# Top-k attention and a GELU MLP on one core: a folded top-k search, softmax rows transposed by row halves ahead of the scores, and GpSimd divisions by two multiplications

## The chip, the cores and the metric

The kernel runs on one core of one Trainium2 chip. The metric is the device time of one execution in microseconds (us), the median of several runs. The engines are named as the profile names them: PE is TensorE (matmuls; PEld are its weight loads), DVE is VectorE, ACT is ScalarE, POOL is GpSimd, SP is SyncE, which here only issues transfers.

## The reference

The first block is attention with a top-k mask; the second is a two-layer MLP with exact GELU over the same tokens. All of q, k, v are float32; w_in and w_out come as 8-byte floats.

```python
batch, n_heads, seq, head_dim = (8, 8, 576, 64)     # q, k, v
n_tokens, d_model, d_ff = (4608, 512, 2048)         # x, w_in, w_out

scores = scale * np.matmul(q, k.transpose(0, 1, 3, 2))
kth = np.partition(scores, -32, axis=-1)[..., -32:-31]
scores = np.where(scores >= kth, scores, -1e9)
attn = np.exp(scores - np.max(scores, axis=-1, keepdims=True))
attn = attn / (np.sum(attn, axis=-1, keepdims=True) + 1e-9)
out = np.matmul(attn, v)
x = out.transpose(0, 2, 1, 3).reshape(4608, 512)
h = x @ w_in
g = 0.5 * h * (1 + erf(h / sqrt(2)))
result = g @ w_out
```

So for each of 64 heads and each of its 576 rows, the 32nd largest of 576 scores is the threshold. Only its value is needed, and the largest score for the exponent.

## The kernel before

**Items and slots.** Heads are taken in pairs. An item is one block of 128 query rows for both heads of a pair, so 128 partitions by 2 x 576 scores. The 64 rows that are left over in each head (576 = 4 x 128 + 64) of two pairs are put together in "last" items. A batch of 8 heads gives 18 items, 16 of the main kind and 2 last ones; all eight give 144 (`items`). The main loop `for n in range(ahead)` has a slot for each item and four more, and in slot n it works on items at different stages: scores of item n+2, search of item n, softmax and division of item n-1, transposes of item n-2, and the product with v of item n-3. The order of the instructions of each engine is the order in which the code issues them; nothing reorders them.

**What one slot issues.** `scores(n + 2)`: matmuls of the last 64 keys of both heads (`t_ps`, L290) and of the 512 main keys (`s_ps`, L294, 64 rows of the array for each head), and ScalarE's copies out of PSUM (L304, L305) into the tile `s`. `attend(n - 3)`: for every second main item, and for each last one, the product with v (`o`, L473 and L484); its copy into the ring `xT` is put on a list and issued by `copy_x()`. `transposes(n - 2)`: eight 128x128 transposes (L436) and one of the last keys (L418) through PSUM, copied to SBUF by ScalarE (L443, L419). `softmax(n - 1, e)` for the two heads e: Prelu pushes what is below the threshold far down (L386), Exp gives the weights and their sum (L387). `top_k(n)`: four rounds of VectorE's MAX8 (L347), which gives the eight largest of a row, and three of MATCH_REPLACE8 (L350), which takes them out; one of each for each head. `inverse(n - 1)`, a reciprocal on VectorE (L373) behind the last round. `threshold(n)` and `add_small(n - 1)`, tiny instructions on GpSimd (L362, L365, L379). `normalise(n - 1)`: the division of the rows of `s` by their sum, two GpSimd instructions (L399), in a few slots on VectorE.

**The MLP** is cut into pieces of some 0.86 us of TensorE work each, in one list. Eight pieces of the first layer (`h_ps`, L525) and eight of the second (`y_ps`, L561) take turns. `mlp(count)` issues the next pieces; a slot issues eight of them, four in slots 10 and 11. So an even slot has a product with v and the first layer, an odd one the second layer. The gelus (L536) of two first-layer units are released behind the sixth piece of the second-layer block (`GELU_AT = 5`) and issued to ScalarE at the next `run_gelus()`. Exp and Gelu each need a table load of their own on ScalarE (`ACT_TABLE_LOAD`).

**PSUM** has eight banks: `s` two, `l1` two (h), `l2` two (y), and the tag `tp` two, which are handed out in turn to `t_ps`, `o` and the transposes. A tile that gets a bank waits until the copy out of the tile before it in that bank is done.

**The first 20 slots** also bring the weights in: units of 8-byte floats come by DMA and are turned into float32 by ScalarE and GpSimd instructions (L190 to L225; L210 multiplies by 2**-13). Up to slot 9 TensorE gets dummy matmuls between its work (`keep_busy`). `START` is 10. Behind the last slot the pieces of the MLP that are left run by themselves.

**Loads.** q and k of a pair come in six transfers each (`load`, L99), the first pair's k by ScalarE's queue and the rest by SP's.

Of the kernel before, what the change touches and what calls it, by code (L numbers as in the profile page):

```python
# [8 lines left out]
TOPK = 32  # L9
# [5 lines left out]
def kernel(  # L15
# [19 lines left out]
    nc = tc.nc  # L35
# [49 lines left out]
    def raw_of(n, pair):  # L85
        return raws[n][pair % len(raws[n])]

    def load(n, pair, queue=None, queue2=None):
        if pair >= n_pairs:
            return  # L90
        queue = queue or nc.sync
        queue2 = queue2 or queue
        b, h0 = pair // NP, 2 * (pair % NP)
        t, src = raw_of(n, pair), sources[n]
        if n != "v":
            for e, a in ((0, 0), (0, 1), (1, 0), (1, 1)):
                at = e * D + a * SQ
                for lo, hi, c in ((0, S, 0),) if e == 0 else ((0, SM, 0), (SM, S, SM + TL)):
                    (queue if a == 0 else queue2).dma_start(  # L99
                        out=t[at : at + SQ, c : c + hi - lo].rearrange("p (j d) -> p j d", d=SQ),  # L100
                        in_=src[b, h0 + e, lo:hi, a * SQ : (a + 1) * SQ].rearrange(
                            "(j p) d -> p j d", p=SQ
                        ),
                    )
            return
        for e in range(2):
            queue.dma_start(
                out=t[:, 0:NM, e, :], in_=src[b, h0 + e, 0:SM].rearrange("(t p) d -> p t d", p=P)
            )
            queue2.dma_start(out=t[e * TL : (e + 1) * TL, NM, e, :], in_=src[b, h0 + e, SM:S])  # L110

    load("k", 0, nc.scalar)
    load("q", 0)
    make_identity(nc, ident)


# [36 lines left out]
    def load_weights(n, queue=None):  # L153

        queue = queue or nc.sync
        u = unit_in(n)
        if u is None:
            return
        src, r, c, dst = weights_of(u)
        if src.dtype == f32:  # L160
            for x in range(2):
                queue.dma_start(
                    out=dst[:, x], in_=src[(r + x) * P : (r + x + 1) * P, c : c + WS]
                )
            return


        half, i = src.bitcast(u16), ORDER.index(u)
        if i not in (2, 12, 14, 15):
            at = FT // 2 + 4 * (i % 2)  # L170
            t = w_out_sb[:, at : at + 4, :].rearrange("p (a b) n -> p a (b n)", a=2)
        else:
            t = stage.tile([P, 2, 2 * WS], f32, tag="words", name="words")
        for a in range(2):
            queue.dma_start(
                out=t[:, a].bitcast(u16)[:, 0 : 4 * WS - 1],
                in_=half[(r + a) * P : (r + a + 1) * P, 4 * c + 1 : 4 * (c + WS)],
            )
        words[u] = t

    def parts(u):

        t, dst = words[u], weights_of(u)[3].bitcast(i32)
        return t[:, :, 0::2], t.bitcast(mybir.dt.int16)[:, :, 2::4], t[:, :, 1::2].bitcast(i32), dst

    def weights_size(u):
        if u not in words:
# [18 lines left out]
    def weights_add(u):  # L206
        if u in words:
            w, _, below, d = parts(u)
            if on_pool(u):
                nc.gpsimd.tensor_scalar(  # L210
                    w.bitcast(i32), w.bitcast(u32), 2.0**-13, None, op0=ALU.mult
                )
            nc.gpsimd.tensor_tensor(d, d, below, op=ALU.add)
            if not ends_late(u):
                weights_end(u)
        made.add(u)
# [60 lines left out]

        return spread(t[:, e * TL :], step + (TL if e == 0 else -TL), TL)

    def scores(i):  # L280
        if i >= N:
            return
        pair, t = items[i]
        S_of[i] = s = work.tile([P, 2 * S], f32, tag="s", bufs=5, name="s")
        s_ps = ps.tile([P, 2, 512], f32, tag="s", bufs=1, name="s_ps")
        t_ps = ps.tile([P, 512], f32, tag="tp", name="t_ps")
        if t < NM:
            qk = qk_of[pair]
            lhsT = qk[:, t * P : (t + 1) * P]
            nc.tensor.matmul(t_ps[:, 0:P], lhsT=lhsT, rhs=qk[:, KT:], start=True, stop=True)  # L290
            for c in range(2):
                for e in range(2):
                    rows = slice(e * D, (e + 1) * D)
                    nc.tensor.matmul(  # L294
                        s_ps[:, e, c * 256 : (c + 1) * 256], lhsT=lhsT[rows, :],
                        rhs=qk[rows, KM + c * 256 : KM + (c + 1) * 256], start=True, stop=True,
                    )
            if i == 0:

                nc.scalar.activation(s[:, 0:SM], s_ps[:, 0], func=AF.Copy, scale=scale)  # L300
                nc.vector.tensor_scalar(s[:, SM : S + TL], t_ps[:, 0:P], scale, None, op0=ALU.mult)
                nc.scalar.activation(s[:, S + TL :], s_ps[:, 1], func=AF.Copy, scale=scale)  # L302
                return
            nc.scalar.activation(spread(s, S + TL, SM), s_ps, func=AF.Copy, scale=scale)  # L304
            nc.scalar.activation(s[:, SM : S + TL], t_ps[:, 0:P], func=AF.Copy, scale=scale)  # L305
        else:
            for r in range(2):
                qk = qk_of[pair + r]
                for e in range(2):
                    nc.tensor.matmul(  # L310
                        t_ps[half(r, e), r * TL : (r + 1) * TL],
                        lhsT=qk[:, SM + e * TL : SM + (e + 1) * TL],
                        rhs=qk[:, KT + e * TL : KT + (e + 1) * TL],
                        start=True, stop=True,
                    )

            for r in range(2):
                qk = qk_of[pair + r]
                for e in range(2):
                    rows = slice(e * D, (e + 1) * D)  # L320
                    nc.tensor.matmul(  # L321
                        s_ps[half(r, e), r, :], lhsT=qk[rows, SM + e * TL : SM + (e + 1) * TL],
                        rhs=qk[rows, KM:KT], start=True, stop=True,
                    )
            s2 = s.rearrange("p (r n) -> p r n", r=2)
            nc.scalar.activation(s2[:, :, 0:SM], s_ps, func=AF.Copy, scale=scale)
            nc.scalar.activation(
                s2[:, :, SM:S], t_ps[:, 0:P].rearrange("p (r n) -> p r n", r=2),
                func=AF.Copy, scale=scale,
            )  # L330

    def top_k(i, hooks):

# [5 lines left out]
            "den": work.tile([P, 2], f32, tag="den", name="den"),  # L339
            "rden": work.tile([P, 2], f32, tag="rden", name="rden"),  # L340
        }
        cur = [row(i, e) for e in range(2)]
        rest = work.tile([P, 2, S], f32, tag="rest", bufs=1, name="rest")
        n_op = 0
        for r in range(TOPK // 8):
            for e in range(2):
                nc.vector.max(st["top"][:, e, 8 * r : 8 * r + 8], cur[e])  # L347
            if r < TOPK // 8 - 1:
                for e in range(2):
                    nc.vector.match_replace(  # L350
                        rest[:, e], st["top"][:, e, 8 * r : 8 * r + 8], cur[e], LOWEST
                    )
                cur = [rest[:, e] for e in range(2)]
            if r in hooks:
                hooks.pop(r)()

    def threshold(i):

# [30 lines left out]
            accum_out=st["den"][:, e : e + 1],  # L389
        )  # L390

    def normalise(i, on_dve):

        if i < 0 or i >= N:
            return
        st = stat_of[i]
        for e in range(2):
            s = row(i, e)
            (nc.vector if e >= 2 - on_dve else nc.gpsimd).tensor_scalar(  # L399
                s, s, st["rden"][:, e : e + 1], None, op0=ALU.mult  # L400
            )

    pt_now = [None]
# [3 lines left out]
    def transposes(i):  # L407
# [35 lines left out]
            nc.scalar.copy(out=dst, in_=tp.rearrange("p (j n) -> p j n", j=NM))  # L443

        return [tails] + [lambda e=e: main(e) for e in range(2)]

    def copy_x():
        while copies:
# [173 lines left out]
    ready, left = [0], [0]  # L622

    eager = [False]
    staging = ExitStack()
    stage = staging.enter_context(tc.tile_pool(name="stage", bufs=1))

    load("k", 1)
    load("q", 1)
    for n in range(1, 3):  # L630
        load_weights(n)
# [7 lines left out]
            nc.tensor.matmul(warm[:, 0:P], lhsT=m, rhs=m, start=True, stop=True)  # L639

    keep_busy(WARM, idle)
    for pair in range(2):
        for piece in transpose_qk(pair):
            piece()
        if pair == 0:
            scores(0)
            scores(1)

# [6 lines left out]
    for pair in range(2, n_pairs):  # L657
        b, p = divmod(pair, NP)
        for at, piece in zip(first.get(pair, slots_of[b % 2][p]), transpose_qk(pair)):
            prep_in.setdefault(starts[b] + at, []).append(piece)  # L660
    ahead = N + 4
    for n in range(ahead):

        left[0] = 4 if n in (START, START + 1) else 8
        eager[0] = n > N
        if not waits(unit_in(n)):
            weights_add(unit_in(n))
        scores(n + 2)
        product = attend(n - 3)
        late = n > START  # L670
        if n <= START:
# [43 lines left out]
        if n < N:  # L715
# [2 lines left out]
                    piece()  # L718
                inverse(n - 1)

            top_k(n, {3: behind_searches})
        else:
            inverse(n - 1)
        threshold(n)
        u = unit_in(n + 1)

        normalise(n - 1, 2 if on_pool(u) else 0)

        if not waits(unit_in(n + 1)):
            weights_size(unit_in(n + 1))  # L730
# [8 lines left out]
    while done[0] < len(pieces):  # L739
        mlp(1)  # L740
        run_gelus()
    staging.close()


# [30 lines left out]
```

## Time and profile before

| | |
|---|---|
| time, median of 3 runs | 1621.87 us (1621.77 to 1622.47) |
| the profiled execution's own time | 1622.63 us |
| its span, first to last instruction | 1620.9 us |
| granted TensorE clock, mean | 0.987 |
| busy: PE, DVE, ACT, POOL | 98%, 90%, 71%, 41% |
| slots, from one first MAX8 to the next: 4 to 7 | 9.70 us each |
| the same, slots 12, 14, 15 and 16 | 12.2 us each |
| the same, slots 20 to 142, mean | 10.55 us |
| first MAX8 of slot 0; of slot 20; of slot 143 | 13.2; 227.1; 1525.0 us |

A line of a group reads: source line, engine, operation, output tile <- input tiles, shapes, count, then busy time in us, mean duration of one in ns, and the engine's idle time before them with what ended it. A line of a timeline has the start, the length, the engine, the line, the operation, the tiles and how many like instructions were merged. The duration of an instruction includes what the next one overlaps; where instructions follow each other without a pause, the time from start to start is the cost of one.

### The profile page before, as it was taken

The numbers are of one execution on the slowest core, as the hardware profiler recorded it, in microseconds if no ns is written. First come the engines' busy times: TensorE is split into PE (matmuls) and PEld (weight loads), VectorE is DVE, ScalarE is ACT, GpSimd is POOL, SyncE is SP. The second block draws the span as 40 slices with busy tenths as digits, with TensorE's granted clock in tenths as the row PEclk, the third lists the DMA queues.
The fourth block names the chain that finished last, engine by engine and source line by source line (L and its number), as shares of the span: only waits on it lengthen the run. The fifth ranks groups of instructions, "written<-read, shape, count | busy, mean of one in ns | idle before, by whom it ended". The sixth has DMA issues, their size and how long they took to land.

```text
span 1620.9 us, 25358 instructions
## 1 busy us (share of the span) xinstructions
PE 1588.7 (98%) x8864; PEld 1082.8 (67%) x8864; DVE 1460.1 (90%) x3108; ACT 1144.1 (71%) x2038; POOL 663.9 (41%) x758
## 2 busy tenths in 40 slices
PE   6899899999999999999999999999999999999999
PEld 5676476766666667776666667676666666666665
DVE  7999999999999999999999998999999999999800
ACT  4898787777777777777777777777777777777720
POOL 3886754333444333344333344333344333444400
PEclk7999999999999999999999999999999999999999
DMA  6533320011101211012100111002110101000000
GB/s 138 169 93 93 92 58 1 20 32 36 35 1 32 33 24 29 1 29 44 36 16 16 29 30 43 1 21 37 30 36 8 36 1 36 2 14 7 1 13 13
DMA packets 202640, 56.18 MB, mean 35 GB/s; under 512 B 193680, under 2 KB 193936, under 8 KB 202512
## 3 DMA queue, kind: packets, MB, share of 16 engines
q1 hardware_dynamic: 199968, 54.13, 14.5%
q8 instruction: 70, 1.15, 0.3%
q10 hardware_dynamic: 2544, 0.43, 0.1%
q14 instruction: 58, 0.48, 0.1%
HBM read 45.08 MB, written 9.44 MB: 34 GB/s over the span
## 4 chain that ended last, share of the span: by engine, by line
PE 87%; DVE 10%; DMA 1%; SPq 1%; issue 0%; POOL 0%; ACT 0%; DVEq 0%; ACTq 0%; POOLq 0%
PE y_ps L561 30%; PE h_ps L525 30%; PE o L473 8%; PE s_ps L294 7%; PE tp L436 7%; DVE top L347 5%; DVE rest L350 4%; PE t_ps L290 2%; PE o L484 1%; PE tp_t L418 1%; PE s_ps L321 1%; SPq L99 1%; DVE qk L255 1%; DVE s L399 0%; PE t_ps L310 0%
## 5 line engine op out<-in xcount | busy, mean ns | idle before, releaser
L347 DVE MAX8 top<-rest 128x8 f32<-128x576 f32 x864 | 609.2, 746 | 0.0
L525 PE MATMUL h_ps<-xT,w_in_sb 128*128 128x256 f32 (+1 forms) x2560 | 547.5, 361 | 0.0
L561 PE MATMUL y_ps<-w_out_sb,g 128*128 128x512 f32 x1152 | 545.0, 600 | 0.0
L399 POOL TENSOR_SCALAR s<-s,rden 128x576 f32<-128x576 f32 x278 | 477.1, 1726 | 8.6 <-DVE rden L373 8.0
L525 PEld LDWEIGHTS h_ps<-xT,w_in_sb 128*128 128x128 f32 x2560 | 432.7, 191 | 64.2 <-issue 14.8
L350 DVE MATCH_REPLACE8 rest<-top,rest 128x576 f32<-128x576 f32 x576 | 423.2, 742 | 0.0
L379 POOL TENSOR_SCALAR den<-den 128x2 f32<-128x2 f32 x144 | 32.1, 223 | 785.2 <-ACT s L387 784.8
L561 PEld LDWEIGHTS y_ps<-w_out_sb,g 128*128 128x128 f32 x1152 | 198.8, 191 | 187.0 <-issue 186.2
L304 ACT ACTIVATE s<-s_ps 128x1024 f32<-128x1024 f32 x127 | 130.7, 1029 | 177.4 <-PE s_ps L294 177.0
L387 ACT ACTIVATE s<-s,bias 128x576 f32<-128x576 f32 x288 | 223.3, 776 | 12.6
L386 ACT ACTIVATE s<-s,neg 128x576 f32<-128x576 f32 x288 | 224.1, 778 | 0.5 <-POOL neg L362 0.4
L443 ACT COPY pt<-tp 128x512 f32<-128x512 f32 x256 | 147.1, 575 | 101.9 <-PE tp L436 101.3
L350 DVE MATCH_REPLACE8 rest<-top,s 128x576 f32<-128x576 f32 x288 | 211.6, 742 | 0.0
L436 PEld LDWEIGHTS tp<-ident,s 128*128 128x128 f32 x1152 | 143.5, 142 | 89.3 <-issue 57.6
L347 DVE MAX8 top<-s 128x8 f32<-128x576 f32 x288 | 201.5, 741 | 0.0
L436 PE MATMUL tp<-ident,s 128*128 128x128 f32 x1152 | 174.2, 275 | 3.9 <-ACT pt L419 3.5
L473 PE MATMUL o<-pt,raw_v 128*64 128x256 f32 x1280 | 152.9, 385 | 0.5 <-ACT pt L443 0.5
L294 PE MATMUL s_ps<-qk 64*128 64x256 f32 x1024 | 150.8, 414 | 0.9 <-ACT s L302 0.5
L473 PEld LDWEIGHTS o<-pt,raw_v 128*64 128x64 f32 x1280 | 86.5, 137 | 64.5 <-issue 15.1
L294 PEld LDWEIGHTS s_ps<-qk 64*128 64x128 f32 x1024 | 91.1, 192 | 23.6 <-ACT s L302 0.8
L536 ACT ACTIVATE g<-h_ps 128x512 f32<-128x512 f32 x144 | 78.6, 594 | 37.8 <-PE h_ps L525 37.1
L387 ACT ACT_TABLE_LOAD x67 | 86.0, 1283 | 5.1
(72 smaller groups left out, 1002.9 us busy)
## 6 DMA issues: line engine op xcount, KB each, us to landing
raw_v<-in_v_dram SPq DMA_DIRECT2D x64, 128.0 KB, 2.4
out_dram<-y SPq DMA_DIRECT2D x31, 256.0 KB, 2.2
w_out_sb<-in_moe_w_in_dram SPq DMA_DIRECT2D x14, 511.8 KB, 4.9
w_out_sb<-in_moe_w_out_dram SPq DMA_DIRECT2D x10, 511.8 KB, 4.1
raw_q<-in_q_dram SPq DMA_DIRECT2D x64, 72.0 KB, 2.2
raw_k<-in_k_dram SPq DMA_DIRECT2D x62, 72.0 KB, 2.3
raw_q<-in_q_dram SPq DMA_DIRECT2D x64, 64.0 KB, 2.2
raw_k<-in_k_dram SPq DMA_DIRECT2D x62, 64.0 KB, 2.2
```

The lines of the kernel that those rows point to most:

```text
L294: nc.tensor.matmul(s_ps[:, e, c * 256 : (c + 1) * 256], lhsT=lhsT[rows, :], rhs=qk[rows, KM + c * 256 : KM + (c + 1) * 256], start=True, s ...
L304: nc.scalar.activation(spread(s, S + TL, SM), s_ps, func=AF.Copy, scale=scale)
L347: nc.vector.max(st["top"][:, e, 8 * r : 8 * r + 8], cur[e])
L350: nc.vector.match_replace(rest[:, e], st["top"][:, e, 8 * r : 8 * r + 8], cur[e], LOWEST)
L386: nc.scalar.activation(s, s, func=AF.Prelu, bias=st["neg"][:, e, 1:2], scale=1.0, alpha=STEEP)
L387: nc.scalar.activation(s, s, func=AF.Exp, bias=st["bias"][:, e : e + 1], scale=1.0, accum_out=st["den"][:, e : e + 1],)
L399: (nc.vector if e >= 2 - on_dve else nc.gpsimd).tensor_scalar(s, s, st["rden"][:, e : e + 1], None, op0=ALU.mult)
L436: nc.tensor.transpose(tp[:, j * P : (j + 1) * P], s[:, first + j * P : first + (j + 1) * P], ident)
L443: nc.scalar.copy(out=dst, in_=tp.rearrange("p (j n) -> p j n", j=NM))
L473: nc.tensor.matmul(o[e * D : (e + 1) * D, 0:n], lhsT=vt[:, j, e, :], rhs=pt[:, e * NM + j if j < NM else 2 * NM, :], start=(j == 0), stop= ...
L525: nc.tensor.matmul(h_tile(u)[:, i, :], lhsT=w_in_sb[:, ko, f * P : (f + 1) * P], rhs=xT[:, ko, c0 : c0 + n], start=(ko == 0), stop=(ko == ...
L561: nc.tensor.matmul(y_of[sub], lhsT=g_of[u][:, i, sub * P : (sub + 1) * P], rhs=w_out_sb[:, f, :], start=(f == 0), stop=(f == FT - 1),)
```

## The change

- **The search is folded.** `fold(n)` takes each row of 576 as two halves of 288 and writes their elementwise maximum and minimum. The minimum comes from VectorE for the first 20 items, later from GpSimd by an integer addition and a subtraction of the maximum. `top_k` then makes four rounds over the maxima and, beside the last two, two rounds over the minima, with 288 elements each, in place. The 32nd largest is put together from the sorted lists by a `min` of 17 pairs and a `max` reduction. `fold(n + 1)` stands behind the search of slot n for the first 20 items, and ahead of it later.
- **GpSimd divides by two multiplications**, the second by 1.0, in every slot (before, VectorE divided in five slots); the same form is used for L210.
- **From slot 20 on** the order is that of `by_rows`. The transposes take the row halves g apart, 16 with 64 rows each, into two banks, issued just ahead of the main scores; the scores of the last keys and their transposes come later, behind four MLP pieces. `copy_x()` stands between the two softmaxes, `inverse` one round earlier, `normalise` ahead of `threshold`.
- The first loads are spread over three queues, the transposes of pair 1 go behind the first round of slot 0, and the staging tile for the weights' words is gone, its units staged in the ring's end instead.

```diff
-    def load(n, pair, queue=None, queue2=None):
+    def load(n, pair, queue=None, for_tail=None):
...
-                    (queue if a == 0 else queue2).dma_start(
+                    (for_tail if lo else queue).dma_start(
...
-    load("k", 0, nc.scalar)
-    load("q", 0)
+    load("k", 0, nc.scalar, nc.gpsimd)
+    load("q", 0, None, nc.gpsimd)
...
-                    w.bitcast(i32), w.bitcast(u32), 2.0**-13, None, op0=ALU.mult
+                    w.bitcast(i32), w.bitcast(u32), 2.0**-13, 1.0, op0=ALU.mult, op1=ALU.mult
...
+    def fold(i):
+        if i >= N:
+            return
+        two = S_of[i].rearrange("p (e h n) -> p h e n", e=2, h=2)
+        high_of, low_of = HL_of[i] = [
+            work.tile([P, 2, S // 2], f32, tag=t, name=t) for t in ("high_of", "low_of")
+        ]
+        a, b, hi, lo = (t.bitcast(i32) for t in (two[:, 0], two[:, 1], high_of, low_of))
+        nc.vector.tensor_tensor(high_of, two[:, 0], two[:, 1], op=ALU.max)
+        if i < BY_POOL:
+            nc.vector.tensor_tensor(low_of, two[:, 0], two[:, 1], op=ALU.min)
+            return
+        nc.gpsimd.tensor_tensor(lo, a, b, op=ALU.add)
+        nc.gpsimd.tensor_tensor(lo, lo, hi, op=ALU.subtract)
...
+        def round_of(x, dst, last):
+            for e in range(2):
+                nc.vector.max(dst[:, e], x[:, e])
+            if not last:
+                for e in range(2):
+                    nc.vector.match_replace(x[:, e], dst[:, e], x[:, e], LOWEST)
         for r in range(TOPK // 8):
+            round_of(high_of, top[:, :, 8 * r : 8 * r + 8], r == TOPK // 8 - 1)
+            if r >= TOPK // 16:
+                x = r - TOPK // 16
+                round_of(low_of, low_top[:, :, 8 * x + 1 : 8 * x + 9], r == TOPK // 8 - 1)
             if r in hooks:
                 hooks.pop(r)()
...
+        nc.vector.tensor_tensor(both, rising, low_top, op=ALU.min)
+        nc.vector.tensor_reduce(
+            top[:, :, TOPK - 1 : TOPK], both, axis=mybir.AxisListType.X, op=ALU.max
+        )
...
-            (nc.vector if e >= 2 - on_dve else nc.gpsimd).tensor_scalar(
-                s, s, st["rden"][:, e : e + 1], None, op0=ALU.mult
+            nc.gpsimd.tensor_scalar(
+                s, s, st["rden"][:, e : e + 1], 1.0, op0=ALU.mult, op1=ALU.mult
             )
...
+    def row_transposes(i):
...
+        tps = [ps.tile([P, 512], f32, tag="tp", name="tp") for _ in range(2)]
+        for e in range(2):
+            for j in range(NM):
+                at = (e * NM + j) * TL
+                for g in range(2):
+                    rows = slice(g * TL, (g + 1) * TL)
+                    nc.tensor.transpose(
+                        tps[g][:, at : at + TL],
+                        s[rows, first[e] + j * P : first[e] + (j + 1) * P], ident[rows, rows],
+                    )
+        for g in range(2):
...
+            nc.scalar.copy(out=dst, in_=src)
...
-    load("k", 1)
+    load("k", 1, nc.scalar)
...
+    def by_rows(n):
+        left[0] = 8
+        eager[0] = n > N
+        fold(n + 1)
+        product = attend(n - 3)
+        softmax(n - 1, 0)
+        copy_x()
+        softmax(n - 1, 1)
+        add_small(n - 1)
+        mlp(1 if product else 3)
+        tails = row_transposes(n - 2)
+        main_scores(n + 2)
+        ready[0] = n_tok[0]
+        mlp(4)
+        copy = last_keys(n + 2, tails)
+        if copy:
+            copy()
+        run_gelus()
+        mlp(left[0])
+        run_gelus()
+
+        def behind_searches():
+            for piece in prep_in.pop(n, []):
+                piece()
+            inverse(n - 1)
+
+        if n < N:
+            top_k(n, {2: behind_searches})
+        else:
+            inverse(n - 1)
+        normalise(n - 1)
+        threshold(n)
+
+    BY_ROWS = 2 * START
     ahead = N + 4
     for n in range(ahead):
 
+        if n >= BY_ROWS:
+            by_rows(n)
+            continue
...
-        scores(n + 2)
+        if n > 0:
+            scores(n + 2)
```

`main_scores` and `last_keys` are the two halves of `scores`; `last_keys(i, more)` issues the last keys' matmuls, then the transposes of the last keys that `more` holds, into the same bank, and their copy, and returns the copy of the scores.

## The prediction

> **What bounds the kernel now.** I read the page's busy line and chain first, then busy windows, the groups by shape, and the timeline of two neighbouring slots.
>
> ```profile
> PE 1588.7 (98%) x8864; PEld 1082.8 (67%) x8864; DVE 1460.1 (90%) x3108; ACT 1144.1 (71%) x2038; POOL 663.9 (41%) x758
> PE 87%; DVE 10%; DMA 1%; SPq 1%; issue 0%; POOL 0%; ACT 0%; DVEq 0%; ACTq 0%; POOLq 0%
> ```
>
> Windows (length; busy time and count of PE, weight loads, DVE, ACT, POOL; clock, DMA):
>
> ```profile
> 40.00:60.00 20.00, 14.09 (x91) 10.22 (x91) 20.00 (x44) 16.98 (x27) 16.80 (x14) 0.83 0.62 160
> 300.00:500.00 200.00, 200.00 (x1040) 134.95 (x1039) 191.80 (x409) 144.45 (x263) 77.46 (x96) 1.00 0.13 27
> ```
>
> Up to about slot 12 (134 us) VectorE is full and TensorE is not. From 205 us on TensorE is full, at full clock; VectorE has some 5% left. So behind 205 us a microsecond counts only if it is TensorE's own or makes it wait. TensorE's slots (an odd slot from 724.61, an even one from 733.95; above them the narrow product of an earlier slot):
>
> ```profile
> 218.08 1.39 PE L484 MATMUL o<-ptt,raw_v 128*64 128x64 f32 x40
> ...
> 724.61 0.38 PE L290 MATMUL t_ps<-qk 128*128 128x128 f32 x2
> ...
> 730.94 0.60 PE L436 MATMUL tp<-ident,s 128*128 128x128 f32 x4
> 731.38 2.74 PE L561 MATMUL y_ps<-w_out_sb,g 128*128 128x512 f32 x6
> 733.95 0.38 PE L290 MATMUL t_ps<-qk 128*128 128x128 f32 x2
> ...
> 735.33 2.38 PE L473 MATMUL o<-pt,raw_v 128*64 128x256 f32 x20
> 737.64 2.86 PE L525 MATMUL h_ps<-xT,w_in_sb 128*128 128x256 f32 x12
> ...
> 745.64 0.38 PE L290 MATMUL t_ps<-qk 128*128 128x128 f32 x2
> ```
>
> Odd slots (no product, second MLP layer) take 9.34 us, even ones (product, first layer) 11.69, a pair 21.03. Starts lie without a gap: four transposes in 0.44.
>
> **Transposes by row halves.** Now 8 x 0.109 = 0.87 us a slot. New: 16, each half the rows and 64 moving columns, in twos on different rows and banks. That twos overlap is seen in the scores (two 64-row products start 7 ns apart). The nearest row for one two is L484: 40 in 1.39 - 0.10, or 20 twos of 0.06. The loads decide whether that may be taken, as a load of 128 columns stays:
>
> ```profile
> L525 PEld LDWEIGHTS h_ps<-xT,w_in_sb 128*128 128x128 f32 x2560 | 432.7, 191 | 64.2 <-issue 14.8 <-ACT s L305 3.8 <-ACT g L536 0.4
> L436 PEld LDWEIGHTS tp<-ident,s 128*128 128x128 f32 x1152 | 143.5, 142 | 89.3 <-issue 57.6 <-ACT s L387 13.1 <-ACT pt L419 5.6
> L484 PEld LDWEIGHTS o<-ptt,raw_v 128*64 128x64 f32 x640 | 20.0, 138 | 5.3 <-issue 4.0 <-ACT g L536 1.3
> ```
>
> A transpose's load (142 ns) is like L484's load of 64 columns (138), not like h's of 128 (191). I take 0.06: 0.48, a gain of 0.39; the other end is 0.109 a two and no gain. (The Trainium skill, "TensorE: Matmul & The Clock Gate", LDWEIGHTS, speaks against the edit: time goes by columns, not rows, 128 / 1.2 = 107 ns. By it the gain would be nothing and my sum 39 us higher; the loads' 142 against 191 say that transposes load faster than that.)
>
> A change between whole-row and split matmuls costs about 0.1 each way (L290 to the scores takes 0.205 instead of 0.109). Beside the scores the halves need no way of their own, but in even slots the product, now first, does: +0.17. So odd slots gain 0.41, even ones 0.22: 0.63 a pair, x62 pairs (slots 20 to 143) = -39 us, between 0 and -60.
>
> **The copy of x.** Tag tp has two banks in turn. An even slot takes them for o, the first half, the second half: the second half lies in o's bank and waits for copy_x. Behind that wait stand all of TensorE's later matmuls. copy_x now stands behind the first softmax, and that behind the gelus of the odd slot before, which stand behind its last-keys copies. ScalarE's pieces:
>
> ```profile
> 732.92 1.28 ACT L536 ACT_TABLE_LOAD   x1
> 734.22 1.09 ACT L536 ACTIVATE g<-h_ps 128x512 f32<-128x512 f32 x2
> ...
> 737.78 0.37 ACT L478 COPY xT<-o 128x256 f32<-128x256 f32 x1 [0.90 <-PE o L473]
> 738.05 0.78 ACT L386 ACTIVATE s<-s,neg 128x576 f32<-128x576 f32 x1
> 738.91 1.28 ACT L387 ACT_TABLE_LOAD   x1
> 740.20 0.78 ACT L387 ACTIVATE s<-s,bias 128x576 f32<-128x576 f32 x1
> 740.88 0.19 ACT L387 ACTIVATION_READ_ACCUMULATOR s<-s,bias 128x1 f32 x1
> ```
>
> From T, the start of the odd slot's tail transpose. ScalarE, start to start: tail copy at T+0.31 (as 728.67 to 728.98), +0.16 last copy, +0.30 table load, +1.30 gelus, +0.97 Prelu, +0.86 table load, +1.29 Exp, +0.68 accumulator, +0.10 copy_x, +0.37 its end, +0.05 TensorE: T+6.39. TensorE: tail 0.11, last y piece 0.86, entry 0.09, o 2.31, one h piece 0.97, entry 0.10: T+4.44. It waits 1.95 us; where a block ends with y copies (one in four) 0.55 more: 2.1 on average. 62 even slots: +130 us, from 100 (1.6 each) to 160 (2.6). In the kernel before, copy_x stood ahead of the softmax and was done at 738.15, and its bank was wanted at 741.3. The stall runs from TensorE's own T, so no faster engine ahead of it takes it away.
>
> **Folded search.** The shortest slots, 9.70 us, are eight MAX8 of 0.66 and six replacements of 0.725. Between the 8-wide MATCH_VALUE_LOAD (0.06) and 576 (0.66) a 288-wide one is 0.36: 12 x 0.36 + 8 x 0.425 = 7.7, fold 0.66 from slot 20 on (twice that before), the two small ones at the end 0.2 to 0.4: 8.7 and 9.4 against 9.63. From slot 20 VectorE isn't the bound (8.7 + 0.4 for reciprocal and its share of the transposes, against 11 us a slot), so that gain is worth nothing there; up to slot 12 it is 12 x 0.2 = -2. A new wait: fold(n+1) at a slot's head waits for slot n-1's last-keys copy, and top_k(n) is queued behind it; from that copy (T+0.77) fold, search, threshold end 0.7 + 8.0 + 0.5 later, still 1 to 2 us ahead of the softmax that needs it: zero, and up to 1 us an odd slot if VectorE is 2 us slower than worked here. Unknown is what two-operand instructions cost beside GpSimd. The nearest row is VectorE's division in the weight slots:
>
> ```profile
> 145.20 1.65 DVE L399 TENSOR_SCALAR s<-s,rden 128x576 f32<-128x576 f32 x2
> 156.67 0.95 DVE L399 TENSOR_SCALAR s<-s,rden 128x576 f32<-128x576 f32 x2
> ```
>
> The first pair ran 0.2 us behind the start of a 2.95 us GpSimd instruction, the second before it: up to 0.7 lost a meeting. One meeting a slot of 0 to 0.7 in 12 slots: 0 to +8, I take +4. (The skill's "SBUF — State Buffer", Who interferes with whom, lets the loser wait out the whole instruction; the first pair would then have ended at 148.9, and it ended at 146.85. By the page 12 slots would lose about 12 x 1.5 = 18 us.)
>
> **GpSimd.** Each slot gains an integer addition and subtraction. 1024 wide is 2.41 us and 2 wide 0.20: 1.44 at 576, so 2.9 a slot. The two-multiplication form isn't in the trace: from half to twice the 1.73, and I take 1.73. 2.9 + 3.45 + 0.65 = 7.0 a slot, hidden in 11. In its queue the division (from the inverse, now 2 us ahead of the search's end) stands before threshold, which it delays by 1.5 us; softmax has that to spare, as ScalarE comes out of the gelus later. The divided rows are there some 5 us ahead of the transposes a slot later. In slots 12 to 16 VectorE loses its division (1.0 to 1.7 each, in 12.2 us slots): 0 to -8, GpSimd taking 11.9 there; I take -2.
>
> **Loads.** K and q lose an issue each from their queue (0.6 us), a k load moves from SP to ScalarE's queue ahead of its first table load; first search ready at 13.2 now: -1 to +1, zero.
>
> **Sum.** The profiled execution took 1622.6 (span 1620.9), 0.8 above the median. 1622.6 - 39 + 130 + (-2 + 4 - 2) - 0.8 = 1713.
>
> **The rivals.** *Faster:* copy_x is in time, because the gelus run 2 us earlier or no table is reloaded between them and Exp. For it: ScalarE is only 71% busy, idle ahead of the last-keys copies; against it: 67 reloads ahead of Exp in before, one for each pair of gelus, and a fixed order. Price: no stall, 1713 - 130 = 1583. It decides once the stall falls under 0.63 us an even slot. *GpSimd's two multiplications take twice as long:* from one inverse to the next lie then 6.9 for dividing, 0.45 threshold, 0.1, the softmaxes (4.8 with reload and copy_x in even slots, 3.1 in odd), 0.5 for den and inverse: 11.9 on average against 22.5 / 2 = 11.25, so +0.65 x 124 = +80, 1793. No row speaks for it. *The halves gain nothing*, loads bound: 1713 + 39 = 1752. *The halves don't overlap:* 16 x 0.109 = 1.74 instead of 0.48, x 124 = +156, 1869; against it the 7 ns. *The fold doesn't shorten the search:* nothing lost behind slot 20 as long as VectorE stays under 11.25; it has 10.1 now.
>
> **How the numbers follow.** Forecast 0.69, by its ends of gain, stall and start 1660 to 1750 on its own; faster 0.23; a stall near 0.6, so no difference, 0.02; GpSimd doubled or loads bound 0.04; no overlap 0.02. As cases of both signs hold most of the chance, the range reaches down into the faster case, to 1580, and up to 1750; left out are about half of the faster case and the dearest ones, near 0.2. About 0.2% is what a measurement of this kernel can tell from no change. Faster 0.23, same 0.02, slower 0.75.
>
> **What would show it.** Right: TensorE idle ahead of the half transposes, released by the xT copy, about 2 us in even slots, 100 to 160 in all; TensorE's share falling towards 92%; a table load between gelu and Exp ahead of each copy_x; twos of transposes 0.06 apart; MAX8 of some 0.44; slot pairs near 22.5. Wrong: even slots without that wait, or VectorE full behind slot 20.

## The result and the profile after

The changed kernel takes 1826.79 us (median of 4 runs, 1824.20 to 1830.68) against 1621.98 us before (4 runs, 1621.77 to 1622.47): ratio 1.1265, 95% interval 1.1248 to 1.1282. The direction was forecast, the size was not: 114 us more than the 1713 forecast, and above the range.

The page of the changed kernel. The third line is the clock that TensorE was granted in 40 slices of the span, in tenths of its full clock; the last is the chain of waits, which was followed back only through the last 4% of the span and tells nothing here, so the waits themselves had to be read.

```profile
PE 1665.4 (91%) x9872; PEld 1109.0 (61%) x9872; DVE 1357.2 (74%) x4704; ACT 1134.4 (62%) x2038; POOL 827.6 (45%) x1020
...
PEclk7999999999998999899899889999989899998999
...
PE 4%; ACT 0%; DVE 0%; issue 0%; DVEq 0%
```

TensorE was to fall to 92%, and is at 91%. But it is busy for 1665 us, 77 more than before, although the halves were to take work from it. The windows (length; busy time and count of PE, weight loads, DVE, ACT, POOL; clock, DMA) show why: the clock is 0.95 on average in the first and 0.92 in the second; before it was 1.00.

```profile
300.00:500.00 200.00, 182.95 (x1076) 122.58 (x1076) 155.51 (x540) 125.31 (x230) 92.94 (x118) 0.95 0.12 25
500.00:700.00 200.00, 182.66 (x1124) 117.76 (x1122) 149.50 (x519) 122.64 (x226) 87.98 (x112) 0.92 0.12 24
```

TensorE's waits (in all, times, longest): the two for the copy of x are far ahead of the rest.

```profile
PE tp L535 <- ACT xT L604: 112.4, 55, 2.7
PE tp L535 <- ACT xT L614: 14.1, 8, 2.7
PE t_ps L331 <- DVE both L423: 7.5, 2, 4.8
...
PE h_ps L651 <- ACT xT L198: 3.1, 1, 3.1
```

From start to start of the transposes, less the usual distance, these 63 waits (55 + 8) cost 136.8 us. One of them, by the timeline (start, length, engine, line, operation, count, idle time before and releaser); T, the odd slot's tail transpose, is at 727.81:

```profile
727.81 0.27 PE L552 MATMUL t_ps<-ident,s 128*128 128x128 f32 x1
...
728.12 0.27 ACT L553 COPY pt<-t_ps 128x128 f32<-128x128 f32 x1 [2.88 <-PE t_ps L552]
728.28 0.28 ACT L353 ACTIVATE s<-t_ps 128x128 f32<-128x128 f32 x1
728.58 1.28 ACT L662 ACT_TABLE_LOAD   x1
...
729.88 1.09 ACT L662 ACTIVATE g<-h_ps 128x512 f32<-128x512 f32 x2
...
730.85 0.78 ACT L457 ACTIVATE s<-s,neg 128x576 f32<-128x576 f32 x1
...
731.69 1.28 ACT L458 ACT_TABLE_LOAD   x1
...
732.27 0.27 PE L535 MATMUL tp<-ident,s 64*128 64x64 f32 x1
...
732.99 0.78 ACT L458 ACTIVATE s<-s,bias 128x576 f32<-128x576 f32 x1
...
733.76 0.35 ACT L604 COPY xT<-o 128x256 f32<-128x256 f32 x1
...
734.16 0.70 PE L535 MATMUL tp<-ident,s 64*128 64x64 f32 x15 [1.62 <-ACT xT L604]
...
734.66 1.97 PE L298 MATMUL s_ps<-qk 64*128 64x256 f32 x8
```

ScalarE goes through its queue as worked out and releases TensorE at T+6.35 (forecast T+6.39); TensorE had its first half transpose at T+4.46 (forecast T+4.44). What was not forecast is the last line: eight score products take 1.97 us, where the slot before, in which nothing waits (half transposes and scores), has 1.08:

```profile
722.50 0.71 PE L535 MATMUL tp<-ident,s 64*128 64x64 f32 x16
723.04 1.08 PE L298 MATMUL s_ps<-qk 64*128 64x256 f32 x8
```

The clock in four windows cut where the record of the granted clock changes:

```profile
727.98:731.40 3.42, 3.42 (x25) 1.70 (x24) 2.80 (x9) 3.25 (x6) 2.68 (x2) 1.00 0.00 0
731.40:734.81 3.41, 1.79 (x26) 1.53 (x27) 3.41 (x15) 3.31 (x6) 0.73 (x1) 1.00 0.00 0
734.81:738.23 3.42, 3.42 (x18) 2.77 (x16) 2.86 (x11) 2.85 (x5) 1.72 (x4) 0.50 0.02 5
738.23:741.64 3.41, 3.41 (x32) 3.41 (x32) 0.00 (x0) 0.10 (x1) 0.40 (x2) 1.00 0.00 0
```

In the second window TensorE worked for 1.79 us and was idle for 1.62. Through the third, although it is full of work, it has half its clock, and then all of it again. Behind 205 us the kernel before has no stretch at half clock while TensorE works; the changed one has 48, of 3.4 us (37) and 6.8 us (11), 201.4 us in all. Half of that is lost: 100.7 us. (Every trace here, that of the kernel before too, also has a short record of half clock that begins behind TensorE's last instruction. It costs nothing and is left out here and below.) 48 of the 63 waits are followed by such a stretch, the other 15 are not.

With the forecast's own 39 that makes 1622.6 - 39 + 137 + 101 = 1822 us, against 1826.8. What the 39 really were, the experiments show.

### The profile page after: what moved, and what is told of

Its sections match the earlier page's. It is cut to its first block, busy times and chain, and to the rows that moved or that the text cites. A ratio compares the mean times of both kernels' runs of the same rounds, so it can differ in the third digit from the quotient of the medians.

```text
span 1824.4 us, 29198 instructions
## 1 busy us (share of the span) xinstructions
PE 1665.4 (91%) x9872; PEld 1109.0 (61%) x9872; DVE 1357.2 (74%) x4704; ACT 1134.4 (62%) x2038; POOL 827.6 (45%) x1020
## 5 line engine op out<-in xcount | busy, mean ns | idle before, releaser
L651 PE MATMUL h_ps<-xT,w_in_sb 128*128 128x256 f32 (+1 forms) x2560 | 607.2, 393 | 6.9 <-ACT g L662 3.8
L405 DVE MAX8 top<-high_of 128x8 f32<-128x288 f32 x1152 | 465.9, 446 | 0.0
L408 DVE MATCH_REPLACE8 high_of<-top,high_of 128x288 f32<-128x288 f32 x864 | 376.0, 443 | 0.0
L388 POOL TENSOR_TENSOR low_of<-s 128x576 int32<-128x576 int32 x124 | 241.9, 1950 | 245.8 <-ACT s L353 234.7
L384 DVE TENSOR_TENSOR high_of<-s 128x576 f32<-128x576 f32 x144 | 109.0, 757 | 312.5 <-ACT s L353 295.2
L470 POOL TENSOR_SCALAR s<-s,rden 128x576 f32<-128x576 f32 x288 | 213.2, 752 | 265.7 <-DVE rden L444 255.1
L405 DVE MAX8 low_top<-low_of 128x8 f32<-128x288 f32 x576 | 232.5, 445 | 0.0
L535 PE MATMUL tp<-ident,s 64*128 64x64 f32 x2016 | 114.1, 243 | 126.5 <-ACT xT L604 112.4
L535 PEld LDWEIGHTS tp<-ident,s 64*128 64x128 f32 x2016 | 87.2, 149 | 202.8 <-ACT xT L604 119.9
L389 POOL TENSOR_TENSOR low_of<-low_of,high_of 128x576 int32<-128x576 int32 x124 | 175.0, 1411 | 9.7
```

The lines of the kernel that those rows point to most:

```text
L388: nc.gpsimd.tensor_tensor(lo, a, b, op=ALU.add)
L389: nc.gpsimd.tensor_tensor(lo, lo, hi, op=ALU.subtract)
L405: nc.vector.max(dst[:, e], x[:, e])
L408: nc.vector.match_replace(x[:, e], dst[:, e], x[:, e], LOWEST)
L470: nc.gpsimd.tensor_scalar(s, s, st["rden"][:, e : e + 1], 1.0, op0=ALU.mult, op1=ALU.mult)
L535: nc.tensor.transpose(tps[g][:, at : at + TL], s[rows, first[e] + j * P : first[e] + (j + 1) * P], ident[rows, rows],)
```

## The experiments

Theory A was: a wait for copy_x of 2.2 us in even slots, and behind each the halved clock; the rest of the change is a gain. Its rivals: the clock falls for another reason (the half-height products, a lower load); the wait is of no account and something else in the new order is slow; the halves or the fold don't do what they are for.

**1. copy_x ahead of both softmaxes**, in the changed kernel:

```diff
         product = attend(n - 3)
-        softmax(n - 1, 0)
         copy_x()
+        softmax(n - 1, 0)
         softmax(n - 1, 1)
```

> The changed kernel with copy_x() ahead of the first softmax in by_rows, nothing else. Theory A (TensorE waits for the copy of x, and the idle time it waits lets its clock fall to half): both go, 1826 - 137 of waiting - 102 of clock = 1587, between 1575 and 1605, no half-clock period behind 205 us. Rival B (the half-height transposes and scores lower the clock by themselves): the waits go, the half-clock periods stay, near 1690. Rival C (the row transposes wait for something else that is late as well, the divided rows or the gelus): near 1826.

Measured: 1596.37 us, ratio to before 0.984 (0.9826 to 0.9855). Two lines exchanged places, and 230 us are gone; it is 1.6% faster than the kernel before. What is left of the wait, and the clock:

```profile
PE tp L535 <- ACT xT L604: 3.7, 13, 0.3
```

```profile
300.00:500.00 200.00, 199.14 (x1216) 130.85 (x1215) 181.01 (x630) 147.20 (x267) 105.07 (x136) 1.00 0.14 28
```

13 waits, 6.4 us from start to start, and no half-clock stretch behind 205 us. The row halves are all still there, so it is not they that pull the clock down. Without the waits this kernel would take 1596.4 - 6.4 = 1590.0; every variant of the wait below is held against this. For the changed kernel itself the parts make 1590.0 + 136.8 + 100.7 = 1827.5, against 1826.8.

A plain pair of slots takes 20.46 us here, 0.57 less than the 21.03 before:

```profile
719.34 0.38 PE L331 MATMUL t_ps<-qk 128*128 128x128 f32 x2
...
739.80 0.38 PE L331 MATMUL t_ps<-qk 128*128 128x128 f32 x2
```

But not every pair is a plain one: the mean slot from 20 to 142 takes 10.40 us against 10.55, only 0.3 less a pair.

**2. The wait filled**: nine dummy matmuls ahead of the row transposes wherever there is a product, so that TensorE has work while the copy is late.

```diff
+        for _ in range(fill):
+            nc.tensor.matmul(tps[0][:, 0:P], lhsT=ident, rhs=ident, start=True, stop=True)
...
-        tails = row_transposes(n - 2)
+        tails = row_transposes(n - 2, 9 if product else 0)
```

> The changed kernel with 9 dummy matmuls (about 2.0 us) in even slots just ahead of the row transposes, written to the bank of the first row half, so that TensorE works while it would wait. Theory A: the slot stays as long as the copy of x is late, but the clock no longer falls: 1826 - 102 = 1724, within 15, half-clock periods behind 205 us near none. Rival B: half-clock periods stay, 1826 or a little more. If TensorE's wait were not there for the dummies to fill: 1826 + 62 x 2.0 = 1950.

Measured: 1752.26 us (2 runs), ratio 1.0801 (1.0779 to 1.0823). The copy is as late as ever, TensorE does nothing useful for as long, and yet 75 us are back, as no half-clock stretch is left:

```profile
300.00:500.00 200.00, 198.32 (x1269) 136.96 (x1269) 162.76 (x565) 130.38 (x239) 97.74 (x124) 1.00 0.12 25
```

The sum was 28 us too low in the filling: the dummies took 2.12 us in each of 70 slots, 148.5 in all, 7 slots having no wait and some a shorter one, and 17.6 us of wait stayed. 1590.0 + 148.5 + 17.6 = 1756.1, within 4 us.

**3. The idle time cut short by some 0.8 us**: three dummies instead of nine.

```diff
-        tails = row_transposes(n - 2)
+        tails = row_transposes(n - 2, 3 if product else 0)
```

> This is the changed kernel (1827 us) with three dummy matmuls of 128 columns (about 0.65 us) ahead of the row transposes in the slots with a product, so that the wait for copy_x stays at its place but TensorE's idle time in it is 0.65 us shorter; the last work is done at the same time. Stalls of 1.9 to 3.0 us become 1.2 to 2.3. Theory A (an idle time over about 1.8 us halves the clock for the next 3.4 us or more): only the 13 longest and some of the 16 next still do it, 13 to 29 half-clock periods instead of 49, 27 to 60 us lost instead of 102, and 7 slots without a stall gain 0.65 each: 1757 to 1790 us. Rival (the clock falls for the mean load, whatever the single gap): 1820 to 1832.

Measured: 1754.55 us, ratio 1.0815 (1.0799 to 1.0832). TensorE still waits 63 times, 92.2 us from start to start, and yet only 10 half-clock stretches remain, 17.1 us lost.

```profile
PE tp L537 <- ACT xT L606: 73.0, 55, 1.8
```

1590.0 + 92.2 + 54.7 (dummies) + 17.1 = 1754.0. The expectation erred to the other side: fewer waits trip the clock than their lengths say. In the changed kernel 20 of 27 waits of 1.9 us did, here none of 10. What decides is not the wait's length but where it lies: all changes of the clock in these traces lie on a grid of 3.413 us. Cut on that grid, the traces of the changed kernel and of this one have 58 windows at full clock in which TensorE was idle for 1.62 us or more, and each was followed by half clock; of the windows with up to 1.60 us none was. A wait that is split over two windows does no harm.

**4. Three MLP pieces ahead of the row transposes in every slot** instead of one in the slots with a product, so that TensorE has 1.7 to 1.9 us more to do before it needs the bank.

```diff
-        mlp(1 if product else 3)
+        mlp(3)
```

> The changed kernel with three MLP pieces instead of one ahead of the row transposes of even slots; copy_x stays between the softmaxes. Theory A: two pieces more are 1.72 us of work in a wait of 1.5 to 3.0 (mean 2.2 us), so some 0.45 us a slot stay, 28 in all, and hardly a half-clock period: 1587 + 28 = 1615, between 1590 and 1635. Rival B: near 1715. Rival C (something other than the copy's lateness against TensorE's place): above 1780.

Measured: 1681.69 us, ratio 1.0359 (1.0342 to 1.0377). 38 waits are left, 58.4 us, and 29.0 us are lost to the clock: 1590.0 + 58.4 + 29.0 = 1677.4. The expectation missed the slots whose next piece is a first-layer piece that isn't ready yet. `mlp(3)` issues nothing there, and the transposes follow the product at once:

```profile
731.10 2.38 PE L599 MATMUL o<-pt,raw_v 128*64 128x256 f32 x20
733.41 0.27 PE L535 MATMUL tp<-ident,s 64*128 64x64 f32 x1
736.39 0.70 PE L535 MATMUL tp<-ident,s 64*128 64x64 f32 x15 [2.71 <-ACT xT L604]
```

The 13 waits of 2.98 us are these; 10 halved the clock, none of the 25 shorter ones did (0.7 to 1.7 us). Of its 12 windows with over 1.6 us idle two, at 1.61 and 1.83 us, kept the full clock, so the bound has a blurred edge.

**5. The old kernel with copy_x between the softmaxes**, to see whether that place is bad in itself:

```diff
-        if n <= START:
-
-            softmax(n - 1, 0)
+        softmax(n - 1, 0)
         copy_x()
...
-        if n > START:
-            softmax(n - 1, 0)
```

> The kernel before, with copy_x() between the two softmaxes from slot 11 on (behind the first softmax, ahead of the transposes), nothing else. Theory A: there the copy would end near 740.2 in the slot of the prediction, and its bank is wanted at 741.3, as two to three pieces and the tail transpose lie between: no wait, 1622 within 5. Rival D (the place of copy_x costs by itself, whatever lies between): as in the changed kernel, 1720 to 1860.

Measured: 1634.02 us, ratio 1.0074 (1.0059 to 1.0089). So the late copy is nearly harmless in the old order, where four MLP pieces stand between o and the tile that takes its bank (741.98 to 745.65 us in this trace); in the new order it is one. Of the 12 us over the expected 1622, 10.0 are another wait, of first-layer pieces for the x they read, 13 of 0.77 us on average by their starts:

```profile
PE h_ps L525 <- ACT xT L478: 7.9, 13, 0.6
```

It takes both: the copy behind a softmax, and the transposes only one piece behind o.

**6. Whole-row transposes** in the kernel of the first experiment:

```diff
         for e in range(2):
             for j in range(NM):
-                at = (e * NM + j) * TL
-                for g in range(2):
-                    rows = slice(g * TL, (g + 1) * TL)
...
+                nc.tensor.transpose(
+                    tps[e][:, j * P : (j + 1) * P],
+                    s[:, first[e] + j * P : first[e] + (j + 1) * P], ident,
+                )
```

> This is the kernel with copy_x() ahead of both softmaxes (1596.4 us), but with the eight whole-row transposes of 128 x 128 in place of the sixteen by row halves, at the same place ahead of the main scores. Theory A (the halves are worth 0.33 to 0.39 us in each of 124 slots, as TensorE is full there): 8 x 0.109 = 0.87 instead of 0.54, so 1596 + 41 = 1637 us, from 1630 to 1648. Rival (the halves gain nothing, the loads bound them, and the gain of the reordered kernel comes from its order): 1596, within 4.

Measured: 1637.03 us, ratio to before 1.0095 (1.0082 to 1.0109). Against whole rows at the same place the halves are worth 40.7 us. The whole rows, with the scores behind them at 0.97, against 0.54 for the halves in the changed kernel (722.50 to 723.04):

```profile
738.50 1.04 PE L532 MATMUL tp<-ident,s 128*128 128x128 f32 x8
739.47 1.14 PE L298 MATMUL s_ps<-qk 64*128 64x256 f32 x8
```

It also shows that the new order without the halves is no gain: it is 15 us slower than the kernel before (1621.8), although it has the two multiplications. So a part of the 40.7 us only pays for the new order.

**7. The unfolded search** in the kernel of the first experiment: the old `top_k` in the place of `fold` and the new one.

> This is the kernel with copy_x() ahead of both softmaxes (1596.4 us), but with the old search: four rounds over 576 elements, no fold. Theory A (behind slot 20 TensorE is the bound, and VectorE with 10.1 us a slot stays just under its 10.25): 1596 plus 0 to 15 there plus 2 to 8 in the first slots, 1604 us, from 1597 to 1620. Rival (with TensorE faster, VectorE would be the next bound, and the fold is what lets the halves count): each slot then takes 10.5 or more as before, 1625 or more.

Measured: 1597.23 us, ratio 0.9846 (0.9833 to 0.986); with the fold it was 1596.37. The fold is worth nothing that can be told. VectorE then looks full, and isn't waited for:

```profile
300.00:500.00 200.00, 199.14 (x1216) 130.96 (x1215) 196.25 (x419) 147.91 (x268) 41.43 (x99) 1.00 0.14 28
```

TensorE's 199.14 us are those with the fold, to the hundredth, while VectorE does 196.25 instead of 181.01.

**8. The two multiplications alone**, in the kernel before, in all slots:

```diff
-                    w.bitcast(i32), w.bitcast(u32), 2.0**-13, None, op0=ALU.mult
+                    w.bitcast(i32), w.bitcast(u32), 2.0**-13, 1.0, op0=ALU.mult, op1=ALU.mult
...
-            (nc.vector if e >= 2 - on_dve else nc.gpsimd).tensor_scalar(
-                s, s, st["rden"][:, e : e + 1], None, op0=ALU.mult
+            nc.gpsimd.tensor_scalar(
+                s, s, st["rden"][:, e : e + 1], 1.0, op0=ALU.mult, op1=ALU.mult
```

> This is the kernel before (1622 us) with one part of the change alone: GpSimd divides and scales by two multiplications, in all slots. Theory A (GpSimd's instruction takes 0.75 us instead of 1.73, which counts only in the weight slots 10 to 19, where GpSimd and VectorE were close to full): 1622 - 5 = 1617 us, from 1612 to 1621; the traces's division of VectorE beside it falls away. Rival (GpSimd's time was hidden there too, and the start's 5 us come from the fold): 1622, within 2.

Measured: 1613.72 us, ratio 0.995 (0.9937 to 0.9962), so 8 us less, all of it ahead of slot 20, which begins at 219.2 us instead of 227.1. A division takes 746 ns instead of 1726:

```profile
L399 POOL TENSOR_SCALAR s<-s,rden 128x576 f32<-128x576 f32 x288 | 212.0, 746 | 11.3 <-DVE rden L373 9.9 <-PE o L473 0.7 <-issue 0.2
```

**9. Only what was worth something**: the kernel before, its own start and search, the two multiplications, and from slot 20 on the new order with the halves and copy_x ahead of both softmaxes.

> This takes from the change only what the runs so far showed to be worth something: the kernel before with its own start (loads, staging, order), GpSimd's two multiplications, the old search without a fold, and from slot 20 on the new order with the row halves and copy_x() ahead of both softmaxes. Theory A (the gains add up: the two multiplications give 8 us up to slot 20, which the old start reaches at 219.2 us instead of 221.4 to 222.4, and from there to the end it is 1376 us as in the kernel without the fold): 1594.5 us, from 1591 to 1597, so 1 to 4 below the version with the fold. Rival (the 2 to 3 us that the new start loses belong to the entry into the new order at slot 20, not to the start): 1597, within 2.

Measured: 1593.98 us, ratio 0.9826 (0.9813 to 0.9839), the fastest of all. It reaches slot 20 at 218.9 us, where the changed kernel is at 222.2: the gains add up, and the other edits of the start cost some 3 us. This run and the eighth experiment have the same start and differ in the order from slot 20 on, so the order with the halves is worth 1613.7 - 1594.0 = 19.7 us, or 26 without the 6.4 us of wait that are left here too. Where the 3 us lie wasn't taken apart. In the changed kernel slots 18 and 19 take 14.6 and 11.2 us instead of 12.2 and 9.7 in the eighth experiment, and TensorE's wait of 3.1 us for L198, shown above, is there: a ScalarE read of weight words that are now staged in the ring's end, before first-layer pieces may use it.

## Why the prediction was wrong

- **The step that failed is the sum, 1622.6 - 39 + 130 - 0.8.** It charges a wait with its own length alone and takes the clock as given. The term that is missing, 101 us, is the halved clock behind 48 of the 63 waits. The clock was read (1.00 from 300 to 500 us, 0.83 at the start) and not asked what had lowered it. Before's own trace has the answer, behind TensorE's wait of 3.57 us for GpSimd at 114.6:

```profile
116.00:120.00 4.00, 1.81 (x5) 1.42 (x6) 4.00 (x10) 3.91 (x8) 4.00 (x3) 0.62 0.35 56
120.00:124.00 4.00, 4.00 (x15) 3.38 (x15) 4.00 (x9) 2.17 (x6) 2.95 (x3) 0.53 0.00 0
```

  A stretch of 6.8 us at half clock follows, 3.4 us lost, and the same behind the other long wait, 3.1 us from start to start at 189.4. With waits of 2 us the size could not be read from before, but the bounds could: 0 to 3.4 us for each of 62 waits, 0 to 211 us, and the range would have reached far above 1750.
- **The wait itself was right**: 136.8 us forecast as 130, its two ends within 0.04 us in the slot shown, in 63 slots for 62. So was the rival on the faster side, in its mechanism: with the copy in time there is a gain, priced at 1583 us and measured as 1596. Its condition was put wrong. It waited for earlier gelus or a spared table load; what decides is copy_x's place against the first softmax.
- **The halves were right in themselves**: 0.067 us a two (0.54 for eight) against 0.06. The rival by which the loads bound them is refuted, and the one by which they don't overlap too.
- **The 39 us were too many.** They stood for the new order with the halves against the kernel before, and that is 26 us without the remaining waits (eighth and ninth experiments). A plain pair gains 0.57 us where 0.63 was forecast, but the forecast took all 62 pairs for plain ones; where the others lose it wasn't taken apart. The start is 5 us better than its forecast of 0, so that the two errors partly cancel, by luck.
- **The fold**: as forecast, nothing behind slot 20, with a MAX8 of 446 ns and VectorE at 74%. The loss to GpSimd, taken as 4 us in twelve slots at up to 0.7 a meeting, came once and was larger:

```profile
62.48 2.41 POOL L231 TENSOR_TENSOR w_in_sb<-w_in_sb,w_out_sb 128x1024 int32<-128x1024 int32 x1
...
63.09 1.85 DVE L423 TENSOR_TENSOR both<-top,low_top 128x34 f32<-128x34 f32 x1
```

  The `min` of 17 pairs takes 0.15 to 0.27 us in the other slots of the start; in this one, slot 4, it began 0.6 us behind a GpSimd addition and ended 0.05 us behind its end. The slot takes 11.2 us, against 9.7 without the fold in the eighth experiment. Slots 1 to 3 take 10.18 us with the fold, 10.41 to 10.43 without it. GpSimd's addition and subtraction take 1.95 and 1.41 us, 3.4 a slot where 2.9 was forecast, and are hidden as forecast.
- **GpSimd's two multiplications were mis-sized**: 1.73 us taken, 0.75 measured (752 ns in the changed kernel), below the lower end of the bound. The start was forecast at 0, and is -5: -8 by the multiplications, +3 by the rest.

## What to carry to other kernels

Price a TensorE wait with the clock that follows it, and look in the trace of before for what its own waits did to the clock; here a wait of 2.2 us cost 3.8. Before a copy out of PSUM is moved behind other work of its engine, work out when the next tile wants that bank, in the new order of the tags. Where a change has several parts, run each alone: here the new order with the halves gave 20 us, the two multiplications 8, the fold nothing, and the place of one line cost 230.

## What the runs showed of the hardware

- The granted clock changes on a grid of 3.413 us. A window in which TensorE was idle for 1.62 us or more, not quite half of it, was followed by one at half clock (58 of 58 in two traces, 10 of 11 in a third); one with less wasn't. A half-clock window with up to 0.13 us idle was followed by full clock (48 in the changed kernel), one with 0.3 us or more by another at half (11). The Trainium skill, "TensorE: Matmul & The Clock Gate", What's actually happening, has such free-running windows of 3413 ns, and the traces agree with 3.413. Its section Why this matters for your kernels warns of idle gaps over some 3 us. Here idle times of 1.62 us (1.9 from start to start) were enough, so the measurement decides: it is the idle share of a window that counts.
- GpSimd's multiplication of 128 x 576 floats by a value per row takes 746 to 752 ns with a second multiplication by 1.0, and 1726 ns without it; of 128 x 1024 integers 1.13 to 1.16 us instead of 2.93 to 3.04. No run here shows why.
- Where a VectorE instruction with two inputs overlapped a GpSimd addition, the one that began later was slowed: the `min` above took 1.85 us instead of some 0.2. From slot 20 on the fold's `max` starts 0.04 us ahead of GpSimd's addition and is not slowed (0.76 us); the addition takes 1.99 us in the 116 slots where they overlap so, and 1.41 where they don't meet.
